# Retention and two feed-forward layers on one core: partial outputs to another pool, no prefetch over the second pass's boundary, stores of left factors from SP's queue

## The chip, the cores and the metric

The kernel runs on one core of a Trainium2 chip. The metric is the device time of one execution in microseconds (us). TensorE (PE) multiplies, VectorE (DVE) and ScalarE (ACT) convert, copy and apply activations, GpSimd (POOL) and SyncE (SP) issue most of the DMA transfers. Each engine works through its own instructions in order.

## The reference

For batch 4, 8 heads, 576 positions and head width 64, 2304 tokens with 512 features in all:

```python
scores = scale * np.matmul(q, k.transpose(0, 1, 3, 2))
ret = scores * Dmat[None, :, :, :]          # gamma ** (i - j) for i >= j, else 0
attn = np.matmul(ret, v)                    # -> x: 2304 tokens x 512
h = x @ w_in                                # 512 x 2048
g = np.where(h >= 1, h, np.where(h <= -1, 0.0, (h + 1) ** 2 / 4))
x = g @ w_out                               # 2048 x 512
out = ((x @ w_a) * (x @ w_b)) @ w_out2      # 512 x 1536, 512 x 1536, 1536 x 512
```

The weights come as float64.

## The kernel before

x stands transposed, 512 features by 2304 tokens, in six blocks of 384 tokens. A float32 product is made of three products of numbers that are split into a high and a low part (`HL`).

**Weights.** A chunk of a weight matrix is loaded as a raw tile of 128 x 512 float64 values (512 KB) into one of four slots of the pool `raw` (`load_raw`, line 140). ScalarE and VectorE turn it into float32 by integer operations (`convert`, lines 152 to 160; line 153 is the first that ScalarE does in the raw tile itself) and split it (`split`). The class `Raws` holds a stream of sources; `more`, after each tile that is taken, begins loads up to two tiles ahead. `raws1` is the stream of the first layer (w_in and w_out of f = 0, 1, ..., 15 in turn), `raws2` that of the second.

**First layer.** The 16 chunks f of 128 hidden features go in three passes i = 0, 1, 2 (`GROUPS1`), each over the blocks b = 0 to 5; the second pass has f = 6 to 10 for all but the first block, the third f = 11 to 15. A step (i, b, f) is twelve matmuls into `ph` (`l1`, out<-in "ph<-x,w"), an activation (`act1`: t on ScalarE lines 494 and 495, on VectorE 496, then its cast into g on ScalarE, line 500, and the rest on VectorE, line 501), and twelve matmuls into four accumulators (`l2`, "acc<-g,w"). `act1` takes t from a pool of four slots. At a block's end `y_out` takes the sums out: in pass 0 it copies them into four tiles `yst` and stores them in DRAM ("y<-yst"), in the later passes it adds them to `yin` tiles that `fetch_y` loaded into the pool `t2` (eight slots) and stores those. Blocks of x go through DRAM too (`fetch_x`, "x<-xd", 1.5 MB).

The retention is done among the steps of pass 0, up to its last but one block; when its 36 units are done (`done[0] == NU`) its pools are closed, the pools `t2`, `y` and others opened, and `side[0]`, the queue for raw loads, changes from SP to GpSimd.

**Second layer's left factors.** Between the steps of the passes `make_more` runs pieces of `maker`: it converts two chunks each of w_a and w_b per pair p (six pairs) into a tile `stage` and forms from it seven tiles q of left factors of a Strassen scheme (cast on ScalarE, line 267, difference on VectorE, line 268), and stores each in DRAM (line 270, 512 KB, names q_0 to q_6). `load_to` loads them again as `w` (line 305, "w<-q", on SP) for the second stage, which begins at about 540 us.

**Order.** A scheduler orders each engine's instructions from the program's order and a simulated timeline. A tile is put into a free slot of its pool; an instruction waits for the readers of what stood in the slot.

Of the kernel before, what the change touches and what calls it, by code (L numbers as in the profile page):

```python
# [9 lines left out]
F32 = mybir.dt.float32  # L10
# [9 lines left out]
P = 128  # L20
TB = 384
# [3 lines left out]
GROUPS1 = [  # L25
    [(0, 4)] + [(0, 6)] * (NB1 - 1), [(4, 11)] + [(6, 11)] * (NB1 - 1), [(11, 16)] * NB1
]
# [54 lines left out]
def retention_ffn_kernel(  # L82
# [12 lines left out]
    nc = tc.nc  # L95
# [3 lines left out]
    NB = B * S // TB  # L99
    NCH = B * S // P  # L100
    NU = NCH * 2
# [4 lines left out]
    tpool = ctx.enter_context(tc.tile_pool(name="t", bufs=4))  # L106
# [6 lines left out]
    def mm(o, l, r, start, stop, goes_on=False):  # L113
        nc.tensor.matmul(o, l, r, start=start, stop=stop, skip_group_check=goes_on)  # L114
# [19 lines left out]
    side = [nc.sync]  # L134
# [8 lines left out]
    def convert(raw, t=None):  # L143


        w = raw.bitcast(U32).rearrange("p (n t) -> p t n", t=2)
        low, high = w[:, 0, :], w[:, 1, :]
        r = raw.bitcast(I32).rearrange("p (n t) -> p t n", t=2)[:, 0, :]
        if t is None:
            t = cpool.tile([P, 512], F32, tag="conv", name="conv")  # L150
        tu, ti = t.bitcast(U32), t.bitcast(I32)
        nc.scalar.activation(t, high.bitcast(F32), AF.Abs, scale=2.0 ** -112)
        nc.scalar.activation(r, low, AF.Copy, scale=2.0 ** -29)  # L153
        nc.vector.tensor_scalar(
            out=tu, in0=tu, scalar1=3, scalar2=None, op0=ALU.logical_shift_left
        )
        nc.vector.scalar_tensor_tensor(
            out=tu, in0=high, scalar=0x80000000, in1=tu, op0=ALU.bitwise_and, op1=ALU.bitwise_or
        )
        nc.vector.tensor_tensor(out=ti, in0=ti, in1=r, op=ALU.add)  # L160
        return t
# [28 lines left out]
    class Raws:  # L190


        def __init__(self, sources):
            self.sources, self.begun, self.taken, self.tiles = sources, 0, 0, {}

        def fetch_to(self, n):
            while self.begun < min(n, len(self.sources)):
                self.tiles[self.begun] = load_raw(self.sources[self.begun])
                self.begun += 1
# [5 lines left out]
            return self.tiles.pop(i)  # L205

        def more(self):
            self.fetch_to(self.taken + 2)

    raws1, raws2 = Raws([src for _, src in stream]), Raws(second)  # L210

    def free():
        return sum(r[1] for r in room.values())

    def take(key):
        r = next(r for r in room if room[r][1] > 0)
        home[key] = r
        room[r][1] -= 1
        return room[r][0]

    def weights_to(n):

        while made[0] < min(n, len(stream)):
            if not free():
                return
            key = stream[made[0]][0]
            weights[key] = split(convert(raws1.next()), take(key))
            made[0] += 1
            raws1.more()

    def used(key):

        weights.pop(key, None)
        room[home.pop(key)][1] += 1
# [4 lines left out]
    qd = [[dpool.tile([P, 2, 512], F32, name=f"q{p}_{k}") for k in range(7)] for p in range(NF2 // 2)]  # L239
# [4 lines left out]
    def maker():  # L244

        for p in range(NF2 // 2):
            if p == LEAD:
                yield from last_tiles(0, 2)
            tiles = {}
            for w in range(2):  # L250
                st = stage.tile([P, 8, 256], F32, tag="stage", name="stage")
                for j in range(2):
                    convert(raws2.next(), st[:, 2 * j:2 * j + 2, :].rearrange("p c f -> p (c f)"))
                    raws2.more()
                    yield
                sub, add = nc.vector.tensor_sub, nc.vector.tensor_add
                add(st[:, S1], st[:, A21], st[:, A22])
                sub(st[:, S2], st[:, S1], st[:, A11])
                sub(st[:, S3], st[:, A11], st[:, A21])
                sub(st[:, S4], st[:, A12], st[:, S2])  # L260
                yield
                for n, o in enumerate(LEFT):
                    k, j = divmod(7 * w + n, 2)
                    if k not in tiles:
                        tiles[k] = take(("m", p, k)).tile([P, 2, 512], F32R, tag="w", name="q")
                    hi, lo = tiles[k][:, j, :256], tiles[k][:, j, 256:]
                    nc.scalar.copy(hi, st[:, o])
                    nc.vector.tensor_sub(lo, st[:, o], hi.bitcast(F32))
                    if j == 1:
                        side[0].dma_start(qd[p][k], tiles[k].bitcast(F32))  # L270
                        used(("m", p, k))
                        banked.add((p, k))
                    if n == 3:
                        yield
                yield
        yield from last_tiles(2, NF2)

    def last_tiles(f0, f1):
        for f in range(f0, f1):
            weights[f] = split(convert(raws2.next()), take(f))  # L280
            raws2.more()
            yield
# [167 lines left out]
    loaded, ready, scored, done = [0], [0], [0], [0]  # L450
# [80 lines left out]
    def y_out(i, b):  # L531
        for m, y in enumerate(ys.pop((i, b))):
            if i == 0:
                t = tpool.tile([P, TB], F32, tag="t", name="yst")
                (nc.scalar.copy if m % 2 else nc.vector.tensor_copy)(t, y[:, :TB])
            else:
                t = yin.pop((b, m))
                nc.vector.tensor_add(t, y[:, :TB], t)
            nc.sync.dma_start((yd[i] if i < 2 else yf)[b][:, m, :], t)
# [182 lines left out]
    ypool = [None]  # L722
# [8 lines left out]
    def needed(step):  # L731
        return place["o", step[2]] + 1

    credit = 0.0
    for s, step in enumerate(steps):
        i, b, f, first, last = step
        f0, f1 = GROUPS1[i][b]
        busy = i == 0 and b < NB - 1
        credit += 0.0 if busy else 1.0 if i == 0 else PACE
        ahead = max(needed(t) for t in steps[s:s + 2 + (not busy)])  # L740
        if made[0] < ahead:
            weights_to(ahead)
            credit = 0.0
        while credit >= 1.0:
            with behind() if i == 0 else nullcontext():
                make_more(2 * GROUPS1[1][0][1] if i == 0 or (i == 1 and b < NB - 2) else len(stream))
            credit -= 1.0
        if first:
            if i == 0:
                x = xt[b]  # L750
            else:
                x = xt.pop((i, b)) if (i, b) in xt else fetch_x(b, xd)
        due = min(UPB * (b + 1) + -(-(f - f0 + 1) * UPB // (f1 - f0)), NU) if i == 0 else NU
        ph, ops = l1(x, weights["i", f])
        for half in (ops[:6], ops[6:]):
            for o in half:
                mm(*o)
            with tc.high_priority(60):
                rounds_to(min(done[0] + 1, due))
        assert done[0] == due  # L760
        if last_use[f] == (i, b):
            used(("i", f))
        gs[step] = act1(ph)
        if prev:
            l2(prev)
        prev = step
        if i == 0 and first:
            nc.sync.dma_start(xd[b], x.bitcast(F32))
        if i == 0 and done[0] == NU and ypool[0] is None:
            att.close()  # L770
            del raw_pools[1:]
            ypool[0] = ctx.enter_context(tc.tile_pool(name="y", bufs=NF2 - 2))
            t2pool = ctx.enter_context(tc.tile_pool(name="t2", bufs=8))
            txpool = ctx.enter_context(tc.tile_pool(name="tx", bufs=5))
            bpool = ctx.enter_context(tc.tile_pool(name="b", bufs=1))
            stage = ctx.enter_context(tc.tile_pool(name="stage", bufs=1))
            side[0] = nc.gpsimd
            room["wx"] = [ctx.enter_context(tc.tile_pool(name="wx", bufs=WBUFS2)), WBUFS2]
        if i > 0 and first:
            fetch_y(i, b)  # L780
        if i == 2 and b == 3 and first:
            load_y(0)
        if i == 2 and b == NB - 1 and first:
            making = right(0)
        if i == 2 and b == NB - 1:
            for _ in range(1 + (not first)):
                next(making, None)
        if f == f0 + 2:
            ni, nb = (i, b + 1) if b + 1 < NB else (i + 1, 0)
            if 0 < ni < 3:  # L790
                xt[ni, nb] = fetch_x(nb, xd)
        if i == 2 and b == NB - 1:
            load_to(9)
# [98 lines left out]
```

## Time and profile before

| | |
|---|---|
| three timed runs | 961.79, 964.97 (median), 966.96 us |
| profiled execution | 965.83 us |
| its span, first to last instruction | 964.1 us |
| mean granted TensorE clock | 0.993 of full speed |

The profiled execution is the one that all rows come from. Its span leaves 1.7 us around the instructions. Busy times are those of instructions on an engine; the idle time before an instruction is named with what ended it ("<-").

### The profile page before, as it was taken

The page shows a single profiled execution, that of the slowest core. Times are in us where ns is not written, and L with a number is a line of the kernel's source. Part 1 is how long each engine was busy: PE and PEld are TensorE (multiplying, and loading weights), DVE is VectorE, ACT ScalarE, POOL GpSimd, SP SyncE. Part 2 cuts the span into 40 slices and gives each one's busy share as a digit, 9 for nine tenths or more (in the row PEclk, how much of TensorE's full clock was granted, in tenths as well). Part 3 has the DMA queues.
Part 4 walks back from the last instruction along what each step waited for, and adds up shares of the span by engine and source line. Part 5 has one row for each costly group of instructions (what it writes and reads, how often), then busy time and mean ns, then how long its engine had stood idle before and what let it go on. Part 6 is the DMA issues. An engine that isn't in the chain of part 4 may idle for free.

```text
span 964.1 us, 16455 instructions
## 1 busy us (share of the span) xinstructions
PE 932.9 (97%) x6188; PEld 920.2 (95%) x6188; DVE 622.9 (65%) x1269; ACT 475.9 (49%) x1022; POOL 94.7 (10%) x148
## 2 busy tenths in 40 slices
PE   6999999999897999999999999999999999999998
PEld 4889989999897999999999999999998999999997
DVE  4899778886587876788968676543345333533332
ACT  2566555564675656667756454433233333433232
POOL 1112110100012210122201000000000000000000
PEclk9999999999998999999999999999999999999999
DMA  9767435333757987799999995648873778548831
GB/s 360 289 231 267 161 129 179 99 138 97 270 180 257 374 318 266 260 348 368 401 409 314 392 318 180 203 143 288 260 250 127 256 261 264 175 165 267 255 105 50
DMA packets 73966, 233.24 MB, mean 242 GB/s; under 512 B 7904, under 2 KB 31136, under 8 KB 71456
## 3 DMA queue, kind: packets, MB, share of 16 engines
q1 hardware_dynamic: 58704, 176.97, 53.0%
q0 software_dynamic: 15040, 55.06, 15.9%
q8 instruction: 49, 0.80, 0.3%
q14 instruction: 29, 0.24, 0.1%
q10 hardware_dynamic: 144, 0.17, 0.1%
HBM read 181.83 MB, written 50.33 MB: 241 GB/s over the span
## 4 chain that ended last, share of the span: by engine, by line
PE 59%; issue 19%; DMA 10%; DVE 8%; ACT 3%; SPq 0%; POOLq 0%; POOL 0%; DVEq 0%; ACTq 0%
PE acc L114 19%; PE ph L114 13%; PE qx L114 9%; PE qy L114 5%; PE late L114 4%; PE po L114 4%; PE qz L114 2%; DMA y<-yst 2%; PE s L114 2%; DMA raw<-in_moe_w_b 2%; DMA raw<-in_moe_w_a 2%; PE pn L114 1%; DMA b<-yf 1%; DMA con<-in_const 1%; DMA xd<-x 1%
## 5 line engine op out<-in xcount | busy, mean ns | idle before, releaser
L114 PE MATMUL acc<-g,w 128*128 128x384 f32 (+1 forms) x1728 | 319.7, 324 | 10.1 <-ACT g L500 7.2
L114 PEld LDWEIGHTS acc<-g,w 128*128 128x128 f32 x1728 | 284.2, 189 | 12.8 <-ACT g L500 8.8
L114 PE MATMUL ph<-x,w 128*128 128x384 f32 x1152 | 223.0, 337 | 3.7 <-DVE t L496 3.4
L114 PEld LDWEIGHTS ph<-x,w 128*128 128x128 f32 x1152 | 202.1, 189 | 5.0 <-DVE t L496 4.0
L114 PE MATMUL qx<-tx,w 128*128 128x288 f32 x1152 | 177.7, 294 | 0.0
L114 PEld LDWEIGHTS qx<-tx,w 128*128 128x128 f32 x1152 | 161.4, 188 | 0.0
L615 ACT COPY keep<-qx 128x288 f32<-128x288 f32 x168 | 66.5, 400 | 139.1 <-PE qx L114 136.0
L114 PE MATMUL qy<-tx,w 128*128 128x288 f32 x576 | 92.1, 295 | 0.0
L114 PE MATMUL late<-g,w 128*128 128x288 f32 x576 | 78.9, 295 | 3.3 <-DVE keep L671 2.2
L114 PEld LDWEIGHTS qy<-tx,w 128*128 128x128 f32 x576 | 81.8, 188 | 0.0
L114 PEld LDWEIGHTS late<-g,w 128*128 128x128 f32 x576 | 76.6, 188 | 4.8 <-DVE keep L671 3.1
L496 DVE SCALAR_TENSOR_TENSOR t<-t,ph 128x384 f32<-128x384 f32 x96 | 52.3, 548 | 33.0 <-ACT t L495 32.6
L494 ACT ACTIVATE t<-ph 128x384 f32<-128x384 f32 x96 | 46.6, 487 | 51.9 <-PE ph L114 47.1
L500 ACT CAST g<-t 128x384 fp32r<-128x384 f32 x96 | 48.8, 510 | 37.5 <-DVE t L496 32.3
L501 DVE TENSOR_TENSOR g<-t,g 128x384 fp32r<-128x384 f32 x96 | 53.1, 556 | 20.8 <-ACT g L500 20.4
L650 DVE TENSOR_TENSOR keep<-keep 128x288 f32<-128x288 f32 x48 | 22.0, 458 | 67.8 <-ACT keep L615 67.7
L153 ACT ACTIVATE raw<-raw 128x512 int32<-128x512 uint32 x68 | 45.7, 674 | 30.1 <-DMA raw<-in_moe_w_b 10.8
L662 ACT CAST g<-keep 128x288 fp32r<-128x288 f32 x56 | 24.2, 433 | 68.3 <-DVE keep L670 29.8
L495 ACT ACTIVATE t<-t 128x384 f32<-128x384 f32 x96 | 50.4, 526 | 1.5
L644 DVE TENSOR_TENSOR keep<-qy,keep 128x288 f32<-128x288 f32 x48 | 21.9, 457 | 39.9 <-PE qy L114 39.9
L114 PE MATMUL qz<-tx,w 128*128 128x288 f32 x288 | 45.9, 294 | 0.0
L346 POOL TENSOR_TENSOR u<-u,con 128x256 f32<-128x256 f32 x36 | 28.1, 781 | 167.0 <-DMA u<-in_qkv 137.2
(85 smaller groups left out, 1121.8 us busy)
## 6 DMA issues: line engine op xcount, KB each, us to landing
w<-q SPq DMA_DIRECT2D x168, 512.0 KB, 4.6
u<-in_qkv SPq DMA_DIRECT2D x36, 640.0 KB, 5.1
q<-q POOLq DMA_DIRECT2D x42, 512.0 KB, 8.4
x<-xd SPq DMA_DIRECT2D x12, 1536.0 KB, 9.7
raw<-in_moe_w_out POOLq DMA_DIRECT2D x21, 512.0 KB, 6.2
xd<-x SPq DMA_DIRECT2D x6, 1536.0 KB, 7.4
yin<-y SPq DMA_DIRECT2D x48, 192.0 KB, 6.3
raw<-in_moe_w_a POOLq DMA_DIRECT2D x12, 512.0 KB, 8.7
```

What stands on the lines that cost most here:

```text
L114: nc.tensor.matmul(o, l, r, start=start, stop=stop, skip_group_check=goes_on)
L153: nc.scalar.activation(r, low, AF.Copy, scale=2.0 ** -29)
L346: nc.gpsimd.tensor_mul(v, v, dec)
L494: nc.scalar.activation(t, ph[:, :TB], AF.Relu, bias=0.5, scale=0.5)
L495: nc.scalar.activation(t, t, AF.Square)
L496: nc.vector.scalar_tensor_tensor(out=t, in0=t, scalar=1.0, in1=ph[:, :TB], op0=ALU.min, op1=ALU.max)
L500: nc.scalar.copy(g[:, 0, :], t),
L501: nc.vector.tensor_sub(g[:, 1, :], t, g[:, 0, :].bitcast(F32)),
L615: nc.scalar.copy(t, o[:, :HT])
L644: nc.vector.tensor_add(self.c12, self.y[:, :HT], self.c12)
L650: nc.vector.tensor_add(self.c22, self.c22, self.s5)
L662: nc.scalar.copy(g[:, 0, :HT], t)
```

## The change

There are three edits. `Raws` gets a list `stops`: at those counts of taken tiles nothing is fetched ahead. For `raws1` they are 21 and 22, which leaves the two tiles of f = 11 (the third pass's first) unfetched at the end of the second pass's weights; the first of them is then asked for at the first step of block 3 of pass 1. The `yst` tiles of the last two blocks of pass 0 (those after the pools are opened) come from `t2`. And the stores of left factors are issued on SP.

```diff
         def __init__(self, sources):
             self.sources, self.begun, self.taken, self.tiles = sources, 0, 0, {}
+            self.stops = ()
@@
         def more(self):
-            self.fetch_to(self.taken + 2)
+            if self.taken not in self.stops:
+                self.fetch_to(self.taken + 2)
 
     raws1, raws2 = Raws([src for _, src in stream]), Raws(second)
+    raws1.stops = (2 * GROUPS1[1][0][1] - 1, 2 * GROUPS1[1][0][1])
@@
                     if j == 1:
-                        side[0].dma_start(qd[p][k], tiles[k].bitcast(F32))
+                        nc.sync.dma_start(qd[p][k], tiles[k].bitcast(F32))
@@
             if i == 0:
-                t = tpool.tile([P, TB], F32, tag="t", name="yst")
+                own, tag = (t2pool, "t2") if done[0] == NU and ypool[0] else (tpool, "t")
+                t = own.tile([P, TB], F32, tag=tag, name="yst")
@@
         busy = i == 0 and b < NB - 1
+        if (i, b, first) == (1, NB - 3, True):
+            raws1.fetch_to(2 * GROUPS1[1][0][1] + 1)
```

GpSimd's queue, from the last weights of the second pass to the first two pairs of left factors (w_in and w_out are of the first layer, w_a and w_b of the second, "q_0_81<-q" is the store of a left factor), before:

```order
L140 DMA raw<-in_moe_w_in 128x4x128
L140 DMA raw<-in_moe_w_out 128x512
L140 DMA raw<-in_moe_w_a 128x4x128 x2
L140 DMA raw<-in_moe_w_b 128x4x128 x2
L140 DMA raw<-in_moe_w_a 128x4x128 x2
L270 DMA q_0_81<-q 128x1024
L270 DMA q_1_82<-q 128x1024
L270 DMA q_2_83<-q 128x1024
L140 DMA raw<-in_moe_w_b 128x4x128
L270 DMA q_3_84<-q 128x1024
L140 DMA raw<-in_moe_w_b 128x4x128
```

and of the change, from the first w_a on (ahead of it stand three pairs of w_in and w_out, where before there were four):

```order
L140 DMA raw<-in_moe_w_a 128x4x128 x2
L140 DMA raw<-in_moe_w_b 128x4x128 x2
L140 DMA raw<-in_moe_w_a 128x4x128 x2
L140 DMA raw<-in_moe_w_b 128x4x128 x2
L140 DMA raw<-in_moe_w_a 128x4x128
L140 DMA raw<-in_moe_w_in 128x4x128
L140 DMA raw<-in_moe_w_a 128x4x128
L140 DMA raw<-in_moe_w_b 128x4x128 x2
L140 DMA raw<-in_moe_w_out 128x512
```

The stores are gone from between the loads, the second pair's two w_b follow its w_a directly, and the pair of f = 11 stands later, with the third pair of left factors.

ScalarE at the first pairs of left factors, in the second pass (lines 494, 495 and 500 are the activation of a step, 153 the conversion in a raw tile, 267 the cast of a left factor), before:

```order
L500 CAST g<-t 128x384
L267 CAST q<-stage 128x256 x2
L153 ACTIVATE raw<-raw 128x512
L494 ACTIVATE t<-ph 128x384
L495 ACTIVATE t<-t 128x384
L153 ACTIVATE raw<-raw 128x512
L500 CAST g<-t 128x384
L267 CAST q<-stage 128x256 x3
```

and of the change, where these lines are 497, 498, 503, 153 and 270:

```order
L503 CAST g<-t 128x384 x2
L153 ACTIVATE raw<-raw 128x512
L165 CAST w<-conv 128x512
L270 CAST q<-stage 128x256 x2
L153 ACTIVATE raw<-raw 128x512 x2
L497 ACTIVATE t<-ph 128x384
L270 CAST q<-stage 128x256 x3
L498 ACTIVATE t<-t 128x384
L270 CAST q<-stage 128x256 x2
L153 ACTIVATE raw<-raw 128x512
L503 CAST g<-t 128x384
```

The two line 153 of the first pair's w_b stand in a row with one of the second pair's, and the line 153 directly ahead of a cast g is that of the second pair's second w_a tile.

SP's queue at the end of pass 0 and the start of pass 1 (line 539 or 543 stores a tile of partial sums, 529 or 532 loads one, 478 or 481 loads a block of x), before:

```order
L529 DMA yin<-y_0_144 128x384
L529 DMA yin<-y_1_145 128x384 x4
L539 DMA y_4_148<-yst 128x384 x4
L478 DMA x<-xd_139 128x3072
L539 DMA y_5_149<-yst 128x384 x4
L478 DMA x<-xd_140 128x3072
L539 DMA y_0_150<-yin 128x384 x4
L529 DMA yin<-y_2_146 128x384 x3
L478 DMA x<-xd_141 128x3072
```

and of the change:

```order
L543 DMA y_4_148<-yst 128x384 x4
L481 DMA x<-xd_139 128x3072
L532 DMA yin<-y_0_144 128x384
L543 DMA y_5_149<-yst 128x384 x4
L532 DMA yin<-y_0_144 128x384 x3
L532 DMA yin<-y_1_145 128x384 x4
L273 DMA q_0_81<-q 128x1024
L273 DMA q_1_82<-q 128x1024
L273 DMA q_2_83<-q 128x1024
L481 DMA x<-xd_140 128x3072
L273 DMA q_3_84<-q 128x1024
```

The loads of yin for blocks 0 and 1 moved behind the stores of blocks 4 and 5, and stores of left factors stand ahead of the next load of x.

## Rows read from the trace of the kernel before

**Rows 1.** The page: busy time, share of the span and instructions of each engine.

```profile
PE 932.9 (97%) x6188; PEld 920.2 (95%) x6188; DVE 622.9 (65%) x1269; ACT 475.9 (49%) x1022; POOL 94.7 (10%) x148
```

**Rows 2.** What PE waited for: us in total, times, longest us.

```profile
PE acc L114 <- ACT g L500: 7.2, 3, 5.7
...
PE ph L114 <- DVE t L496: 3.4, 1, 3.4
```

**Rows 3.** Windows: length, busy PE, PEld, DVE, ACT, POOL, clock, DMA share, GB/s.

```profile
248.00:254.00 6.00, 2.60 (x15) 2.28 (x14) 1.18 (x2) 1.41 (x4) 0.10 (x1) 1.00 0.79 259
294.00:304.00 10.00, 4.29 (x23) 3.97 (x22) 3.54 (x9) 3.16 (x8) 0.75 (x1) 0.93 0.74 274
304.00:312.00 8.00, 8.00 (x33) 8.00 (x33) 7.70 (x18) 7.39 (x17) 2.40 (x4) 0.66 0.75 277
318.00:340.00 22.00, 22.00 (x129) 22.00 (x128) 19.66 (x46) 15.38 (x36) 6.32 (x10) 1.00 1.01 383
440.00:540.00 100.00, 99.98 (x585) 100.00 (x585) 81.32 (x175) 65.43 (x142) 19.68 (x34) 1.00 1.00 378
...
303.00:306.00 3.00, 2.71 (x8) 2.71 (x9) 2.69 (x7) 2.90 (x9) 1.43 (x3) 0.50 0.20 76
```

**Rows 4.** Timeline near 250 us: start, us, engine, instruction [idle before <- releaser].

```profile
244.02 4.76 SPq L539 DMA_DIRECT2D y<-yst  x4
...
251.18 1.00 ACT L494 ACTIVATE t<-ph 128x384 f32<-128x384 f32 x2 [3.28 <-DMA y<-yst]
...
253.23 4.65 PE L114 MATMUL ph<-x,w 128*128 128x384 f32 x24 [3.40 <-DVE t L496]
```

**Rows 5.** Timeline near 300 us.

```profile
291.19 0.32 SPq L478 DMA_DIRECT2D x<-xd  x1
...
292.43 0.75 POOL L140 DMA_DIRECT2D raw<-in_moe_w_b  x1 [1.85 <-ACT q L267]
...
302.19 0.65 ACT L153 ACTIVATE raw<-raw 128x512 int32<-128x512 uint32 x1 [6.81 <-DMA raw<-in_moe_w_b]
...
303.29 4.21 PE L114 MATMUL acc<-g,w 128*128 128x384 f32 x12 [5.71 <-ACT g L500]
...
304.46 1.75 POOL L270 DMA_DIRECT2D q<-q  x3 [8.33 <-DVE q L268]
```

**Rows 6.** Timeline from 408 to 450 us.

```profile
419.24 0.68 ACT L153 ACTIVATE raw<-raw 128x512 int32<-128x512 uint32 x1 [2.86 <-DMA raw<-in_moe_w_b]
...
423.78 2.39 PE L114 MATMUL acc<-g,w 128*128 128x384 f32 x12 [1.19 <-ACT g L500]
...
435.95 0.66 ACT L153 ACTIVATE raw<-raw 128x512 int32<-128x512 uint32 x1 [2.44 <-DMA raw<-in_moe_w_a]
...
440.02 0.58 PE L114 MATMUL acc<-g,w 128*128 128x384 f32 x2 [0.85 <-ACT raw L153]
```

**Rows 7.** GpSimd's stores (busy, mean ns, idle; waits; landing), then landings of raw tiles.

```profile
L270 POOL DMA_DIRECT2D q<-q x42 | 22.7, 542 | 69.5 <-DVE q L268 69.0
...
POOL q L270 <- DVE q L268: 69.0, 32, 12.6
...
q<-q POOLq DMA_DIRECT2D x42, 512.0 KB, 8.4
...
DMA to landing us min/median/max: 3.5/6.8/15.3
```

**Rows 8.** Conversion on VectorE by line: busy us, mean ns | idle before.

```profile
L157 DVE SCALAR_TENSOR_TENSOR conv<-raw,conv 128x512 uint32<-128x512 uint32 x44 | 30.0, 686 | 0.8
...
L154 DVE TENSOR_SCALAR conv<-conv 128x512 uint32<-128x512 uint32 x44 | 19.0, 436 | 9.2 <-ACT conv L152 8.9
```

**Rows 9.** Loads of x on SP after 440 us, and their landings in all.

```profile
449.61 0.66 SPq L478 DMA_DIRECT2D x<-xd  x1
...
490.05 0.32 SPq L478 DMA_DIRECT2D x<-xd  x1
...
DMA to landing us min/median/max: 6.4/8.8/14.6
```

## The prediction

> **What bounds the kernel now.** I read the page's busy times first. TensorE (PE) is busy 97% of the span and the next engine 65% [rows 1], so time can be won only where PE stands still or runs at a lower clock. PE's waits come next [rows 2]. What stands out between the start and the second stage is 7.2 us in three waits for the cast g (the longest 5.7) and 3.4 us once for t. The timeline and a table of windows then give the place and the cause of each.
>
> For a rate I take a stretch in which PE is full and the clock whole: 129 matmuls in 22.0 us [rows 3], 5.86 a microsecond. What a disturbed window lost is its length at that rate, less its own matmuls, divided by the rate.
>
> Place A, 248 to 254 us, lies where the first pass hands over to the second. ScalarE's Relu into t sat 3.28 us until stores y<-yst had landed, and PE then stood 3.40 us for t [rows 4]. The slots that the Relu needed still held copies of the finished block's partial sums, whose four stores were issued at 244.02. The window has 15 matmuls for 35.2: 20.2 / 5.86 = 3.4 us. The clock stayed 1.00.
>
> Place B, 294 to 312 us, lies in the second pass. GpSimd issued the second w_b tile at 292.43; ScalarE's line 153 stood in order for it until 302.19, idle 6.81 us, with the cast g of a step behind it, and PE stood 5.71 us [rows 5]. The two windows hold 23 + 33 matmuls where 18 us would hold 105.5: 49.5 / 5.86 = 8.4 us. The idle time is 5.7 of it; 2.7 belong to the stretch after it, where the granted clock is 0.50 (the 1.2 GHz level): 8 matmuls in 3 us from 303 on, where 17.6 would fit [rows 3].
>
> Place C are 423.78 and 440.02, further on in the second and at the start of the third pass: 1.19 us and 0.85 us of PE, both behind a line 153 that stood for a raw tile (2.86 and 2.44 us) [rows 6]. Together 2.0 us.
>
> A, B and C are 3.4 + 8.4 + 2.0 = 13.8 us, 1.4% of the span, and the most that the change can win by removing waits. The start and the second stage are not touched.
>
> **The change, part by part.** First, the copies of the last two blocks. Eight yst tiles move from the pool that act1 uses (four slots) to t2 (eight slots), which is empty then. The copies themselves cost the same. Only the wait of place A goes: -3.4 us. What is late next are the yin tiles, which now find the t2 slots taken until the eight stores have landed; the order of SP shows their loads behind the stores. They are read when a block of the second pass ends, five steps of 24 matmuls later (5 x 24 / 5.86 = 20 us), and four stores took 4.76 us to issue [rows 4], so I cost this at nothing. If that cover were gone, the price would be that of A again.
>
> Second, the raw tiles. There are four slots. Before, the two tiles of f=11 were fetched at the boundary and lay in two of them while the first two pairs of w_a and w_b went through the other two, so that a w_b tile could be asked for only when an earlier one was through (1.85 us of GpSimd idle before the issue at 292.43 [rows 5]). After, the first two pairs' eight tiles stand on GpSimd with nothing between them, and the casts of q and the lines 153 come at another place. The w_b tiles are asked for a step or more earlier, which is over 4.1 us (24 / 5.86); place B had them late by 6.81 on ScalarE. Added is no instruction: both tiles of f=11 are loaded later, one of them at block 3.
>
> Third, the 42 stores of left factors go from GpSimd to SP. On GpSimd they take 42 x 0.542 = 22.7 us of issue and stand idle for 69.5 us [rows 7], in order, with the raw loads behind them; the issue at 304.46 came only after 8.33 us idle [rows 5]. GpSimd is no bound, so the 22.7 us buy nothing; the in-order standing is what made raw loads late at place C. After, GpSimd only loads. On SP, the stores now stand ahead of loads of x, yin and w.
>
> The row says that a raw load pays for the wait of the store ahead of it. The Trainium skill (DMA: Bandwidth & Descriptors, Issuing engines are not separate DMA queues) says that transfers begun by different engines run on the same 16 DMA engines and that another issuer saves only the time to begin them. By that rule the third edit would save 22.7 us off the path and nothing on it, place C's 2.0 us would stay, and the sum would end 2.0 us higher; the trace goes against it in so far as the 69.5 us are waits for DVE in the issuer's order, not transfers.
>
> **What takes their place.** The trace of before can't show the new order's waits, so this is bounded: nothing below, and 13.8 above (all three places return). Four contributions, each an estimate.
> 1. The second pair's second w_a tile. In the new order line 153 for it stands directly ahead of a cast g (the last rows of the ScalarE piece), as at place B. Its load waits until the pair before has been converted; some ten instructions of 0.4 to 0.7 us each [rows 8] on ScalarE and VectorE, 6.3 us, then a landing of 3.5 us, the shortest [rows 7], or of the 9.76 us from 292.43 to 302.19 [rows 5], then 1.2 us for line 153 and the cast (0.65 + 0.5): 11.0 or 17.3 us. By the order PE has 86 matmuls, 14.7 us, for that time. So 3.7 us to spare or 2.6 us late. The median landing of a raw tile is 6.8 [rows 7], which leaves 0.4 to spare: I take 0.5.
> 2. A q cast now waits until the store of the tile in its slot, from SP, has landed. Between the store and the cast lie some five steps, over 20 us, and a store lands in 8.4 at the median [rows 7]: 0.5.
> 3. Place C stays in part: a lead of two steps is 8.2 us, near the raw tiles' landing of 6.8, with 15.3 the longest [rows 7]: half of it, 1.0.
> 4. The later tiles of f=11: two steps of lead in place of four, with the same landing: 0.5.
> Together 2.5, between 0 and about 6 by the long landings.
>
> **The sum.** The profiled execution took 965.83 us, 1.7 around its span of 964.1. 965.83 - 13.8 + 2.5 = 954.5. The median of the three timed runs is 964.97, 0.86 lower: 953.7 us.
>
> **Rivals.**
> *B moves on.* The wait goes to the next raw tile that stands ahead of a cast g, at B's price (5.7 idle and 2.7 at half clock, less the 2.5 already in): 953.7 + 8.4 - 2.5, about 960. For it: case 1 above is late with the long landing. Against: the long landing had 1.5 MB of x (issued at 291.19 [rows 5]) and the other raw tiles beside it; in the new order the x load of that block stands among the stores.
> *Nothing changes.* From 253 to 443 us the work may be one chain of raw loads, each waiting for a slot, and a gain at A then only makes B longer: about 965. For it: after A every wait of PE in this stretch is for a raw tile or for a cast behind one. Against: in 318 to 340 PE is full [rows 3], so that there is slack between the waits.
> *Slower: x late.* On SP a load of x now stands behind stores that wait for VectorE. From 440 to 540 the DMA engines are full, share 1.00, PE too [rows 3]. The x loads there, the first at 449.61 and the last at 490.05, are issued about a block ahead of their use (five steps, 20 us), and the longest landing of x is 14.6 [rows 9]: some 6 us to spare. Three stores are 1.5 MB, 4 us at the window's 378 GB/s. From 6 us on each further one is PE idle. Four blocks at 2 us each, and 2.7 us of low clock after each, are +19 us: about 972, less what is won there. The deciding point is a load issued 6 us later than before. For it: the standing of the stores was up to 12.6 us [rows 7]. Against: the scheduler placed the loads among the stores in the order, not behind them all. Beside it the Trainium skill (DMA: Bandwidth & Descriptors, Queues, rings and completion order) says that a DMA engine takes packets from its queue rows in turn, so that x would share SP's row with the stores; no row here shows the shares.
>
> **How the numbers follow.** A change of 0.5%, 4.8 us, is about what a measurement here can tell. Forecast, all three places gone but for 1 to 6 us: 0.66, 952 to 958. B moves on: 0.14, around 960, on the edge of what counts as faster. Nothing changes: 0.12, 961 to 967. x late: 0.08, above 969. Faster gets the forecast and half of B: 0.73; same 0.19; slower 0.08. The range goes from all 13.8 won with two runs' scatter below (948.5) to the case of B moved on with a little more (961.5), leaving out most of the last two cases.
>
> **What would show it.** PE's waits lose 3.4 for t and most of the 7.2 for the cast g; the clock shows no 0.50 around 303; the stores y<-yst release no Relu; GpSimd's rows have no q. If the forecast is wrong, a new wait of PE of over 3 us for a cast g or for x stands between 260 and 560 us, with a DMA as the last releaser ahead of it. Up to 240 us and from 560 us on nothing should differ.

## The result, and the profile after

| | before | changed |
|---|---|---|
| median | 964.32 us (961.79 to 966.96, 4 runs) | 949.84 us (947.6 to 954.68, 4 runs) |
| profiled execution | 965.83 us | 947.6 us |
| its span | 964.1 us | 945.8 us |

The ratio is 0.9866, 95% interval 0.9834 to 0.9898: 12.9 us faster (9.8 to 16.0); the two medians lie 14.5 us apart, inside that interval. Forecast were 953.7 us, 11.3 below the median then known, in a range of 948.5 to 961.5.

The page's first part, busy time and share of the span, answers to [rows 1]:

```profile
PE 928.9 (98%) x6188; PEld 918.3 (97%) x6188; DVE 622.5 (66%) x1269; ACT 475.5 (50%) x1022; POOL 72.6 (8%) x106
```

The same work stands in a span 18.3 us shorter, of two single executions. GpSimd has 42 instructions fewer, the stores, and is 22.1 us less busy, which nothing waited for. What PE waited for in the changed kernel (us in total, times, longest), in answer to [rows 2]:

```profile
PE late L114 <- DVE keep L675: 2.2, 4, 0.6
...
PE ph L114 <- ACT w L165: 0.3, 1, 0.3
PE acc L114 <- ACT g L503: 0.3, 1, 0.3
```

The wait for the cast g has 0.3 us for 7.2, the wait of `ph` for t is gone, and so is that for a raw tile. The windows of [rows 3] in the changed kernel (length, busy PE, PEld, DVE, ACT, POOL, clock, DMA share, GB/s):

```profile
248.00:254.00 6.00, 6.00 (x36) 6.00 (x35) 6.00 (x12) 5.67 (x13) 0.75 (x1) 1.00 0.51 176
294.00:304.00 10.00, 10.00 (x60) 10.00 (x59) 8.41 (x19) 6.18 (x14) 0.00 (x0) 1.00 1.02 397
304.00:312.00 8.00, 8.00 (x48) 8.00 (x47) 7.32 (x19) 5.76 (x14) 1.50 (x2) 1.00 0.91 313
303.00:306.00 3.00, 3.00 (x19) 3.00 (x18) 3.00 (x8) 1.32 (x4) 1.43 (x2) 1.00 0.97 324
```

36, 60 and 48 matmuls for 15, 23 and 33, with the clock whole. PE is full here and stays so from 180 to 360 us and from 400 to 600. SP's own waits in the changed kernel show where the standing of the stores went (GpSimd had it for 69.0 us [rows 7]):

```profile
SPq L273 <- DVE q L271: 69.2, 28, 14.1
```

The same 69 us, on another queue. No wait of PE after the start names a load from SP.

### The profile page after: what moved, and what is told of

Same layout as the page of the kernel before. It is cut to its first block, busy times and chain, and to the rows that moved or that the text cites. A ratio compares the mean times of both kernels' runs of the same rounds, so it can differ in the third digit from the quotient of the medians.

```text
span 945.8 us, 16431 instructions
## 1 busy us (share of the span) xinstructions
PE 928.9 (98%) x6188; PEld 918.3 (97%) x6188; DVE 622.5 (66%) x1269; ACT 475.5 (50%) x1022; POOL 72.6 (8%) x106
## 4 chain that ended last, share of the span: by engine, by line
PE 89%; DMA 5%; DVE 4%; ACT 1%; issue 1%; SPq 0%; ACTq 0%; POOLq 0%; DVEq 0%
PE acc L114 27%; PE ph L114 18%; PE qx L114 16%; PE late L114 8%; PE qy L114 8%; PE qz L114 4%; PE po L114 4%; PE s L114 2%; PE pn L114 1%; DMA con<-in_const 1%; DMA raw<-in_moe_w_a 1%; DMA raw<-in_moe_w_out 1%; DMA raw<-in_moe_w_in 1%; DVE conv L157 1%; DMA y<-yst 1%
## 5 line engine op out<-in xcount | busy, mean ns | idle before, releaser
L114 PE MATMUL acc<-g,w 128*128 128x384 f32 (+1 forms) x1728 | 314.5, 322 | 0.5 <-ACT g L503 0.3
L114 PE MATMUL ph<-x,w 128*128 128x384 f32 x1152 | 220.1, 336 | 0.3 <-ACT w L165 0.3
L641 DVE TENSOR_TENSOR keep<-qz,keep 128x288 f32<-128x288 f32 x48 | 21.9, 457 | 36.7 <-PE qz L114 35.6
```

The costliest lines, as they stand in the source:

```text
L641: nc.vector.tensor_add(self.c11, z[:, :HT], self.c11)
```

## The experiments

Eight kernels are the change's three edits in all combinations, each with its own profile; four more take one suspected cause apart. "First" is the prefetch, "second" the copies, "third" the stores' queue, in the order of the change as described ahead of the prediction; the prediction itself takes the copies first and the prefetch second. The ratios are to the kernel before on the same chip, whose medians there were 962.14 to 963.31 us.

| edits | ratio | 95% interval |
|---|---|---|
| none (a second time) | 1.0008 | 0.9988 to 1.0027 |
| first | 1.0032 | 1.0011 to 1.0053 |
| second | 0.9913 | 0.9892 to 0.9934 |
| third | 1.0030 | 1.0012 to 1.0047 |
| first, second | 0.9870 | 0.9845 to 0.9896 |
| second, third | 0.9913 | 0.9889 to 0.9938 |
| first, third | 1.0011 | 0.9985 to 1.0038 |
| all (a second time) | 0.9859 | 0.9833 to 0.9885 |

The second edit is the only one that gains alone, 8.4 us. The first adds 4.1 us to it (0.9913 to 0.9870). The third adds nothing that can be told, with the second or with both; 2.0 us, the forecast for it, is about as much as the intervals can tell there. Without the second, the others gain nothing.

**The kernel before, once more.** No edit.

> The kernel before once more, with a second profile: how far the same program's waits scatter. Expected: places A, B and C again, each within 1 us of the first profile; the 2.0 us for a copy at 121 us and the 1.1 us for g in the second stage may be gone or moved, as they are no part of the change.

Measured: 964.38 us (959.94 to 967.1), a profile with a span of 959.7. Its windows of 20 us (117 matmuls fit in one), at places A, B and C:

```profile
240.00:260.00 20.00, 16.98 (x89) 16.66 (x88) 10.47 (x20) 11.06 (x24) 1.28 (x3) 0.91 0.72 255
...
300.00:320.00 20.00, 17.64 (x93) 17.32 (x92) 16.27 (x38) 15.76 (x36) 5.30 (x9) 0.91 0.91 319
...
420.00:440.00 20.00, 18.89 (x109) 18.59 (x108) 16.24 (x38) 11.52 (x28) 5.26 (x8) 1.00 0.98 346
```

They lose 28, 24 and 8 matmuls: 4.8, 4.1 and 1.4 us at 5.86 a microsecond, 10.3 together. The prediction took 3.4, 8.4 and 2.0 from shorter windows and waits of the first profile; in windows like these that profile has 95 at A, 102 and 80 at B (280 to 320) and 102 at C, losses of 3.8, 8.9 and 2.6 us. The expectation of 1 us was clearly missed at B, and about met at A and C. At B the raw tile issued at 293.84 was in by 301.89, when line 153 began, after 8.05 us where the first profile had 9.76, and PE's wait was 2.36 us for 5.71. At A the clock dipped, which it had not done before. So what one profile prices at 8.4 us is 4.1 in the next.

**The changed kernel, once more.** No edit.

> The changed kernel once more. Expected 12 to 15 us faster than before (1.2 to 1.5%), PE without a wait of over 1 us from 180 to 600 us. If the first profile was a lucky one (947.6 us, the fastest of four runs), a wait of 1 to 5 us for a cast g or a raw tile shows in this one.

Measured: 949.29 us (948.01 to 952.83). Between 180 and 600 us PE has one wait, of 0.9 us for a cast g. The first profile was no lucky one.

**Second edit alone.**

```diff
-                t = tpool.tile([P, TB], F32, tag="t", name="yst")
+                own, tag = (t2pool, "t2") if done[0] == NU and ypool[0] else (tpool, "t")
+                t = own.tile([P, TB], F32, tag=tag, name="yst")
```

> The second edit alone (the copies of the last two blocks from the other pool). If the three places are independent: place A's 3.4 us go, so about 0.35% faster, the wait for the cast g at place B (some 5.7 us, with half clock after it) is still there. If the work from 253 us on is one chain of raw loads: no difference in time, and the wait at place B is longer than 5.7 us by up to 3.4.

Measured: 953.67 us, ratio 0.9913, more than either reading in the expectation gave (3.4 us or nothing). A is gone (117 matmuls from 240 to 260), C too (117 from 420 to 440), and B is there, with 97 and 113 matmuls in its two windows, 24 lost. The timeline at B (start, us, engine, instruction [idle before <- releaser]):

```profile
286.22 0.75 POOL L140 DMA_DIRECT2D raw<-in_moe_w_a  x1 [2.48 <-ACT raw L153]
286.27 0.32 SPq L478 DMA_DIRECT2D x<-xd  x1
...
295.59 0.65 ACT L153 ACTIVATE raw<-raw 128x512 int32<-128x512 uint32 x1 [5.34 <-DMA raw<-in_moe_w_a]
...
296.69 3.08 PE L114 MATMUL acc<-g,w 128*128 128x384 f32 x12 [2.47 <-ACT g L500]
```

It is another tile than before, a w_a, but the same meeting: a raw load of 0.5 MB begun within 0.1 us of a load of x of 1.5 MB takes 9.4 us until line 153 can start. In the first profile the two were 1.2 us apart [rows 5].

**First edit alone.**

```diff
+            self.stops = ()
...
-            self.fetch_to(self.taken + 2)
+            if self.taken not in self.stops:
+                self.fetch_to(self.taken + 2)
...
+    raws1.stops = (2 * GROUPS1[1][0][1] - 1, 2 * GROUPS1[1][0][1])
...
+        if (i, b, first) == (1, NB - 3, True):
+            raws1.fetch_to(2 * GROUPS1[1][0][1] + 1)
```

> The first edit alone (no raw tiles fetched ahead over the boundary). If the places are independent and the two tiles of f=11 in the raw slots are what makes place B: 8.4 us faster (0.9%), no half clock near 300 us, the 3.4 us for t at place A and the 2.0 us of place C still there. If the stores among the raw loads make place B too: a wait of several us for a cast g stays between 290 and 330 us and the gain is under 4 us.

Measured: 964.91 us, ratio 1.0032. The place came out as expected and the time did not. B's windows are full:

```profile
280.00:300.00 20.00, 20.00 (x117) 20.00 (x116) 18.23 (x40) 16.87 (x38) 5.43 (x8) 1.00 0.62 205
300.00:320.00 20.00, 20.00 (x118) 20.00 (x117) 17.57 (x42) 12.62 (x30) 5.23 (x9) 1.00 1.01 377
```

A stays, with 83 matmuls and a clock of 0.83 from 240 to 260. In place of B stand new waits: 1.57 us at 329, 2.61 us at 411, 2.14 us at 538 for a copy of ScalarE. The one at 411:

```profile
399.76 0.76 POOL L140 DMA_DIRECT2D raw<-in_moe_w_a  x1 [4.37 <-DVE conv L160]
400.16 0.32 SPq L481 DMA_DIRECT2D x<-xd  x1
...
409.36 0.65 ACT L153 ACTIVATE raw<-raw 128x512 int32<-128x512 uint32 x1 [5.91 <-DMA raw<-in_moe_w_a]
...
411.06 1.68 PE L114 MATMUL ph<-x,w 128*128 128x384 f32 x8 [2.61 <-DVE t L499]
```

The same meeting once more, 0.4 us apart, at a later block: 9.6 us for the raw tile. The window of C, 420 to 440, is full (118 matmuls).

**Third edit alone.**

```diff
-                        side[0].dma_start(qd[p][k], tiles[k].bitcast(F32))
+                        nc.sync.dma_start(qd[p][k], tiles[k].bitcast(F32))
```

> The third edit alone (stores of left factors from SP). If the places are independent: place C's 2.0 us go (0.2%), A and B stay as they are. If only the sequencer's time of the issues counts, as the skill's rule has it: no difference and place C stays. If loads of x pay for the stores ahead of them: slower, with PE waiting for x.

Measured: 964.69 us, ratio 1.0030. C did not go, it grew, from 102 matmuls to 85 (5.5 us lost):

```profile
420.00:440.00 20.00, 15.82 (x85) 15.53 (x84) 13.58 (x32) 10.15 (x25) 3.01 (x4) 0.93 0.89 327
```

```profile
421.03 0.75 POOL L140 DMA_DIRECT2D raw<-in_moe_w_a  x1 [11.41 <-ACT q L267]
421.04 0.32 SPq L478 DMA_DIRECT2D x<-xd  x1
...
431.81 0.67 ACT L153 ACTIVATE raw<-raw 128x512 int32<-128x512 uint32 x1 [4.69 <-DMA raw<-in_moe_w_a]
...
437.50 0.98 PE L114 MATMUL acc<-g,w 128*128 128x384 f32 x2 [4.18 <-DVE yin L538]
```

GpSimd's load had no store ahead of it; GpSimd stood idle for 11.41 us until a cast of a left factor on ScalarE, then the load met x and took 10.8 us. PE's wait is put down to the addition into yin on VectorE; that came late because VectorE had stood for t, and ScalarE, which makes t, for this raw tile. PE never waited for x.

**First and second edit.** The first two diffs above together.

> First and second edit, the stores left on GpSimd. If the places are independent: 3.4 + 8.4 = 11.8 us faster than before (1.2%), some 2 us slower than the whole change, with waits like place C's between 400 and 450 us. If the stores' standing among the loads is what matters most: under 6 us faster, with waits for a cast g behind a raw tile.

Measured: 948.9 us, ratio 0.9870, and the view of PE's waits is empty between 180 and 600 us. The stores stand among the raw loads as before, and place C is not there.

**Second and third edit.**

> Second and third edit, the prefetch over the boundary left in. If the places are independent: A and C go, 3.4 + 2.0 = 5.4 us faster than before (0.6%), place B's wait for a cast g with its half clock stays. If the stores on SP alone free the raw loads at place B too: over 10 us faster and no half clock near 300 us.

Measured: 954.65 us, ratio 0.9913. B is there (4.43 us of PE at 301, and a clock of 0.84 from 300 to 320, in the slowest of the six runs), A and C are not. For the waits that is as the expectation for independent places had it; the gain is 8.4 us rather than 5.4.

**First and third edit.**

> First and third edit, the copies of the last two blocks left in the activation's pool. If the places are independent: 8.4 + 2.0 = 10.4 us faster than before (1.1%), 3.4 us slower than the whole change, with the 3.4 us wait of PE for t at the first boundary. If the places are one chain: as fast as the whole change within 1 us in spite of that wait.

Measured: 964.36 us, ratio 1.0011, against both readings in the expectation. A stays (93 matmuls), B is full but for 5, and two other windows lose 22 and 35 matmuls, 9.7 us:

```profile
320.00:340.00 20.00, 18.03 (x95) 17.74 (x94) 16.11 (x37) 13.38 (x29) 2.25 (x3) 0.91 0.95 336
400.00:420.00 20.00, 15.87 (x82) 15.55 (x81) 13.16 (x31) 12.44 (x30) 2.25 (x3) 0.91 0.76 252
```

Both stand behind a raw tile of w_a that was issued 0.8 and 1.2 us after a load of x (313.88 after 313.13, 400.64 after 399.47).

**Loads of x of half the bytes.** Two kernels, on before and on first and third edit. What they leave out: the low part of x in the second and third pass.

```diff
-        nc.sync.dma_start(t.bitcast(F32), space[b])
+        nc.sync.dma_start(t[:, 0].bitcast(F32), space[b][:, 0])
...
-                ops.append((ph[:, :TB], w[:, a, ws], x[:, z, cc, :]))
+                ops.append((ph[:, :TB], w[:, a, ws], x[:, z * low[0], cc, :]))
...
+        low[0] = int(i == 0)
```

> The kernel before, with loads of x of half the bytes (0.75 MB): the low parts are not loaded in the second and third pass, and the matmuls take the high part in their place, so the output is not the reference's. If the wait at place B is a raw tile that lands late because 1.5 MB of x were begun within some 3 us of it (landings of 8 to 9.4 us there in five profiles), that raw tile lands in 5 to 6.5 us, line 153 waits under 3 us in place of 5.2 to 6.8, PE's wait for the cast g goes, and 4 to 9 us are won; place A stays. If the slots that the prefetched tiles hold are the cause, as the prediction had it: the wait of line 153 stays within 1 us.

> First and third edit, with loads of x of half the bytes as in the run before this one (same part left out). There PE's new waits stood at 327 and 411 us, each behind a raw tile of w_a issued next to a load of x. If x is the cause: both waits go, place A's alone stays, and it is 5 to 10 us faster than first and third edit with whole loads (0.99 to 0.995 of before). If something else in that order is the cause: waits of 2 to 4 us stay there, and the time with them.

Measured: 975.14 us, ratio 1.0134 (1.0094 to 1.0173), and 970.32 us, ratio 1.0088 (1.0054 to 1.0123): slower, against every expectation of the time. In the first of them place B keeps its instructions, and reads as expected if the load of x is what makes the tile late:

```profile
293.40 0.75 POOL L140 DMA_DIRECT2D raw<-in_moe_w_b  x1 [1.86 <-ACT q L267]
293.54 0.32 SPq L478 DMA_DIRECT2D x<-xd  x1
...
299.51 0.67 ACT L153 ACTIVATE raw<-raw 128x512 int32<-128x512 uint32 x1 [3.16 <-DMA raw<-in_moe_w_b]
...
300.63 1.68 PE L114 MATMUL acc<-g,w 128*128 128x384 f32 x8 [0.70 <-ACT g L502]
```

6.1 us for the raw tile in place of 8.05 and 9.76, and 0.70 us of PE in place of 2.36 and 5.71. In the second kernel the w_a tile that met x at 313 took 5.48 us until line 153 (314.60 to 320.08), where first and third edit had 10.95 (313.88 to 324.83). But PE's wait there did not go, as it was expected to: 2.41 us for 1.97, now behind the next tile, one of w_in, that took 10.4 us beside a load of x of half the size:

```profile
314.60 0.75 POOL L140 DMA_DIRECT2D raw<-in_moe_w_a  x1 [13.48 <-ACT q L270]
315.38 0.38 SPq L481 DMA_DIRECT2D x<-xd  x1
316.14 0.75 POOL L140 DMA_DIRECT2D raw<-in_moe_w_in  x1 [0.79 <-DVE q L271]
...
326.56 0.66 ACT L152 ACTIVATE conv<-raw 128x512 f32<-128x512 f32 x1 [3.91 <-DMA raw<-in_moe_w_in]
...
328.23 0.62 PE L114 MATMUL acc<-g,w 128*128 128x384 f32 x2 [2.41 <-ACT g L505]
```

The other wait, 4.13 us at 411, is gone; one of 1.03 us stands at 406 behind a tile that no load of x met. And between 180 and 600 us both kernels have more waits for a cast g, eight and ten, 11.1 and 16.5 us in all, where the first profile of before had two, 6.9 us. The longest in the first, 3.58 us at 368.90, stands behind a tile of w_in that was issued at 358.64, 0.64 us ahead of a load of x, and was in only at 367.23. So a load of half the size made two tiles land earlier and left others as late as before. The order behind it is another too, so these two kernels tell about those tiles and not about the time of the change.

**Second edit for one block.**

```diff
-                own, tag = (t2pool, "t2") if done[0] == NU and ypool[0] else (tpool, "t")
+                own, tag = (t2pool, "t2") if done[0] == NU and ypool[0] and b == NB - 2 else (tpool, "t")
```

and with `b == NB - 1`.

> The second edit for block 4 only: the copies of block 5 stay in the activation's pool. Place A lies at the end of block 4 by the stores at 244 us, so that A's 3.4 to 5 us go here. If that wait is all of the second edit, this gives its whole gain (8.4 us, 0.9%). If block 5's copies are what else counts: 3 to 5 us.

> The second edit for block 5 only. Place A's wait of PE for t stays (3 us and more). If block 5's copies make the rest of the second edit's gain: 3 to 5 us faster than before, with place C gone. If place A is all: no difference beyond 0.3%.

Measured: 959.93 us, ratio 0.998 (0.9951 to 1.0008), for block 4; 955.51 us, ratio 0.993 (0.9905 to 0.9954), for block 5. Place A is gone in both, 117 matmuls from 240 to 260, which was not expected for block 5; nor was it expected that block 4's copies alone gain next to nothing and block 5's 6.7 us. Why A is gone with block 5's is on SP's queue. Before:

```profile
236.62 1.27 SPq L529 DMA_DIRECT2D yin<-y  x3
...
238.41 5.51 SPq L529 DMA_DIRECT2D yin<-y  x5
244.02 4.76 SPq L539 DMA_DIRECT2D y<-yst  x4
```

With block 5's copies alone moved:

```profile
240.42 7.30 SPq L540 DMA_DIRECT2D y<-yst  x4
```

Eight loads of yin stood ahead of the four stores, five of them for 5.5 us, and the slots of t were not free until the stores had landed. When block 5's copies take slots of t2, those loads move behind the stores, and the stores begin 3.6 us earlier. So that move is enough for A, with block 4's copies still in the slots of t. When block 4's copies are in t2, they don't hold slots of t at all; but there too the loads of yin stand behind the stores (from 245.39), so that no run shows the slots alone.

The kernel with block 4's copies alone has a worse C, 75 matmuls from 420 to 440 and PE waiting 5.74 us at 437, and again a raw tile at a load of x (this profile is of the slowest of its twelve runs, 965.89 us, so it shows more than is usual there):

```profile
419.63 0.52 SPq L478 DMA_DIRECT2D x<-xd  x1
419.67 0.77 POOL L140 DMA_DIRECT2D raw<-in_moe_w_a  x1 [4.72 <-ACT q L267]
...
431.88 0.67 ACT L153 ACTIVATE raw<-raw 128x512 int32<-128x512 uint32 x1 [7.22 <-DMA raw<-in_moe_w_a]
```

That with block 5's alone has 118 there. So C follows the order that an edit happens to give.

## Why the prediction was right

**The sum held, its split did not.** That PE's lost time lies at three places, that all three can go, and that little takes their place was right: 13.8 less 2.5 forecast, 12.9 measured. Which edit removes which place, and what makes B and C, was only partly right. By the runs the second edit alone gives 8.4 us where 3.4 were forecast for it, the first adds 4.1 to it for 8.4, and the third about 1, within the intervals, for 2.0. That the sum came out in spite of this is in part luck: the errors cancelled.

**Place A.** Right: the Relu waited for slots that copies of partial sums held, and the second edit removes it. Wrong: the place lies at the end of block 4, one block ahead of the change of passes, as the stores there are block 4's. Missing: the eight loads of yin ahead of the stores. The prediction saw these loads move and costed that at nothing; by the run with block 5's copies that move is itself enough to remove A. The term of 3.4 us was small: in the profiles that have A it is 24 to 34 matmuls from 240 to 260 where the clock dips with it, 4.1 to 5.8 us, and 3.8 in the first.

**Place B.** Right: the prefetch is what B needs. With whole loads of x, the kernels with the first edit lose at most 6 matmuls from 280 to 320, and those that keep the prefetch lose 24 or more. Right too that the tiles are asked for earlier, and by far more than a step: the first pair's second w_b was asked for at 292.43 before, at 272.72 in the changed kernel, 13 us ahead of that block's load of x (285.93). Mis-sized: 8.4 us came from one profile; the second of the same program has 4.1, and the first edit adds 4.1 to the second. The cause named, slots held by the two tiles, is not the whole of it. In all seven profiles that have the prefetch and whole loads of x, the late tile was issued within 1.3 us of a load of x and took 8 to 11 us until line 153; with half the bytes of x it took 6.1. What the meeting is made of shows on the DMA engines, here in the first profile (a window as in [rows 3]):

```profile
293.00:301.00 8.00, 4.58 (x27) 4.25 (x25) 3.81 (x10) 1.58 (x3) 1.67 (x3) 1.00 0.99 367
```

They are full, share 0.99. From 291.19 to 295.38 a load of x and three raw tiles were begun, 3.15 MB in all, which at 367 GB/s is 8.6 us (an estimate), near the 9.76 of the tile. So x is half of these bytes and raw tiles are the other half; the w_in tiles that were late beside a load of x of half the size show that x alone does not settle a landing. That x makes the tile at B late is supported by the one profile with half of it; that the two meet at this place only with the prefetch is what the profiles with and without it show.

**Place C.** This step failed: "the in-order standing is what made raw loads late at place C", worth 2.0 us to the third edit. With the stores moved alone C grew to 5.5 us and the kernel was 0.3% slower; with the first or the whole second edit C's window is full, wherever the stores stand, though with the first and without the second a wait stands at 411 instead. The Trainium skill (DMA: Bandwidth & Descriptors, Issuing engines are not separate DMA queues) says that another issuer saves only the time to begin the transfers. That rule, which the prediction set aside, fits better: GpSimd's busy time fell by 22.1 us, the 69 us of standing went along to SP, and the third edit's part in the time is 0.9870 to 0.9859, inside the intervals.

**What takes their place.** 2.5 us were forecast. Between 180 and 600 us the two profiles of the changed kernel show no wait of PE and one of 0.9 us; from 360 to 400 us, where 234 matmuls fit, they have 230 and 224, a loss of 0.7 and 1.7 us. The raw tile at 289.33, the second pair's first w_b, still lands late, 8.4 us after its issue and 3.4 us behind a load of x, but without harm. In the changed kernel:

```profile
285.93 0.75 SPq L481 DMA_DIRECT2D x<-xd  x1
...
289.33 0.75 POOL L140 DMA_DIRECT2D raw<-in_moe_w_b  x1 [8.70 <-DVE t L499]
...
294.75 4.32 PE L114 MATMUL ph<-x,w 128*128 128x384 f32 x24
...
297.70 0.67 ACT L153 ACTIVATE raw<-raw 128x512 int32<-128x512 uint32 x1 [2.77 <-DMA raw<-in_moe_w_b]
298.27 0.50 ACT L503 CAST g<-t 128x384 fp32r<-128x384 f32 x1
```

ScalarE stood 2.77 us, and a cast g stands right behind that line as at place B. PE did not stand, as it had 24 matmuls of `ph` to do from 294.75 on. The cover is thin: PE's next matmuls for `acc` began at 298.91, just after that cast. In the second profile line 153 began there at 299.74 and ScalarE stood 3.79 us, and PE lost about one matmul (116 from 300 to 320). So the changed kernel covers B's wait; it does not rule it out. Contribution 1 was late in neither profile.

**The rivals.** "B moves on" lost for the whole change and happened in its parts: with the first edit, or the first and third, the wait moved to 411 us (2.6 and 4.1 us of PE). "Nothing changes" lost; its chain of loads, where a gain at A only lengthens B, is refuted by the second edit alone, which kept its gain. "x late" lost: no profile has PE waiting for x. Where x does harm, it is to the raw tiles beside it.

**What stays open.** Why the first edit gains only with the second. In the profiles the difference is where raw loads meet loads of x. The first pair's second w_b, asked for at 292.43 before, is asked for at 286.23 with the first edit, at 281.45 with the second, at 282.56 with the first and third, and only with the first and second together at 272.64. Each edit changes the scheduler's order behind it, and no run holds the order while one cause is changed. The first profile also lost about 2 us at 121 us and 1.1 us in the second stage, which other profiles of the same program share or lack; of the 18.3 us between the two first spans some 3 are such scatter.

## What to carry to other kernels

When a stall is a late transfer, look at what was issued within a microsecond of it on the other queues before blaming the slot or the queue that it came by. Run edits alone before crediting each with a stall: with a scheduler between code and order, three edits here gave -0.9, +0.3 and +0.3% alone and -1.4% together. A stall that depends on a landing should be priced from two profiles; one said 8.4 us, the next 4.1.

## What the runs showed that was not expected

At the places read here, where a raw tile of 0.5 MB was issued from 0.4 us ahead of a load of x of 1.5 MB to 1.3 us behind it, ScalarE's line 153 started 8 to 12 us later; raw tiles land in 6.8 us at the median and 3.5 at best [rows 7]. A little more lead was enough: in the first profile the w_b tile issued at 289.82, 1.4 us ahead of the load of x at 291.19, was in by 293.77. Loads of half the bytes made the kernel 1.3 and 0.9% slower, by waits at other places.
